# Block-sparse attention and Fourier mixing on one core: idle products before the first scores, first copies of q on ScalarE, and transposes left for the next slot

## Chip, cores and metric

The kernel runs on one core of a Trainium2 chip. The metric is the device time of one execution, in microseconds (us), as the median of three runs.

## The reference, cut to what matters

```python
def _attn_ref(q, k, v, sampled_blocks):          # q, k, v: (4, 8, 768, 64)
    scores = 1/sqrt(64) * np.matmul(q, k.transpose(0, 1, 3, 2))
    # mask: neighbouring blocks of 32, first and last block, 3 sampled blocks a row
    scores = np.where(mask, scores, -1e9)
    attn = softmax(scores)                       # + 1e-9 in the denominator
    return np.matmul(attn, v)

def _moe_ref(x, w_ch1, w_ch2):                   # x: (4, 768, 512)
    mixed = np.real(np.fft.fft(np.fft.fft(x, axis=1), axis=2))
    u = x + mixed
    un = (u - mean(u)) / np.sqrt(var(u) + 1e-6)  # over the last axis
    ch = np.maximum(un @ w_ch1, 0.0) @ w_ch2     # 512 -> 2048 -> 512
    return u + ch

def reference(...):
    attn_out = _attn_ref(q, k, v, sampled_blocks)
    x = attn_out.transpose(0, 2, 1, 3).reshape(4, 768, 512)
    return _moe_ref(x, w_ch1, w_ch2)
```

## The kernel before

The order of instructions on every engine is fixed when the program is generated: the kernel is a Python generator that lays out one static program, and each engine then runs its instructions in that order, waiting where data or a buffer is not there yet. To choose the order, the generator keeps a rough clock of its own (`when`, `free`: estimates in us of when an engine or a PSUM bank is free). These estimates are not times of the chip.

The attention is laid out in slots. A pair of heads `n` takes six slots, `s` = 0 to 5; a batch (four pairs) takes 24, and `r` is the slot's number within the batch. There are 4 x 24 slots and one more for the last remainder. A slot issues the scores of two units (a unit is 128 keys against 384 queries, for two heads), their exponentials, and the products with v of the slot before. In the first batch (`phase` 0) the mask enters as a small extra matmul and the row sums are taken on TensorE (`add_up`); in the later ones VectorE multiplies with a mask and GpSimd adds up. From the second batch on, the Fourier and channel work of the batch before fills TensorE between the slots (`apart`, `late`).

Besides these there are **short steps**: `turn` transposes a piece of q or k on TensorE and copies it out of PSUM; `place` transposes a finished half of the attention output into x; `total` takes row sums; `mask_step` builds a piece of the mask. Nearly all use one of two PSUM tags: `t`, which has a single bank, or `m`, which has two.

The parts that the change and the steps of the prediction touch (cuts marked):

```python
    sum_p = ctx.enter_context(tc.tile_pool(name="sum_p", bufs=1))
    # ... cut ...
    ps_t = ctx.enter_context(tc.tile_pool(name="ps_t", bufs=1, space=PSUM))
    ps_m = ctx.enter_context(tc.tile_pool(name="ps_m", bufs=2, space=PSUM))
    # ... cut ...
    when = {"PE": 0.0, "ACT": 0.0, "DVE": 0.0, "POOL": 0.0}
    free = {"m": [0.0, 0.0], "t": [0.0]}
    # ... cut ...
    def busy(engine, us, after=0.0):
        when[engine] = max(when[engine], after) + us
        return when[engine]
    def bank(tag):
        at = free[tag].index(min(free[tag]))
        when["PE"] = max(when["PE"], free[tag][at])
        free[tag][at] = float("inf")
        return tag, at
    def give(which, at):
        free[which[0]][which[1]] = at + HOP
    # ... cut: a warm-up product, and the first transposes of q and k ...
    def warm(n):
        m = ps_m.tile([P, P], FP32, tag="m", name="warm")
        for _ in range(n):
            nc.tensor.matmul(m, ident, ident, start=True, stop=True)
    # ... cut ...
    def w_round(i):
    # ... cut ...
        nc.scalar.mul(out=lo.bitcast(FP32), in_=lo, mul=2.0 ** -52)
        nc.scalar.mul(out=a.bitcast(FP32), in_=hi.bitcast(FP32), mul=2.0 ** -112)
        nc.vector.tensor_scalar(out=a, in0=a, scalar1=3, scalar2=0x7FFFFFFF,
                                op0=ALU.logical_shift_left, op1=ALU.bitwise_and)
        nc.vector.scalar_tensor_tensor(out=dst.bitcast(U32), in0=hi, scalar=0x80000000, in1=a,
                                       op0=ALU.bitwise_and, op1=ALU.bitwise_or)
        nc.vector.tensor_scalar(out=a, in0=dst.bitcast(U32), scalar1=0xFF800000, scalar2=None,
                                op0=ALU.bitwise_and)
        nc.vector.tensor_mul(out=a.bitcast(FP32), in0=lo.bitcast(FP32), in1=a.bitcast(FP32))
        nc.vector.tensor_add(out=dst, in0=dst, in1=a.bitcast(FP32))
        busy("DVE", 3.0, busy("ACT", 1.2))
    # ... cut ...
    def turn(n, a, half):
        t = loaded[n, a]
        if half == 0:
            turned[n, a] = tp_p.tile([P, S], FP32, tag="qk"[a] + "T", name="qk"[a] + "T")
        dst = turned[n, a]
        first = n == 0 and half == 0
        tag, pool = ("m", ps_m) if first and a == 0 else ("t", ps_t)
        tp, at = pool.tile([P, 512], FP32, tag=tag, name="tp"), bank(tag)
        if a == 0:
            parts = [t[:, c // 2, c % 2, :, :] for c in (range(4, 6) if half else range(4))]
        else:
            parts = [t[:, T * half + c, :, :] for c in range(T)]
        for c, part in enumerate(parts):
            nc.tensor.transpose(tp[:, c * P:(c + 1) * P], part, ident)
        done = busy("PE", 0.15 * len(parts)) + HOP
        if a == 1:
            nc.scalar.copy(out=dst[:, half * HS:(half + 1) * HS], in_=tp[:, 0:HS])
            give(at, busy("ACT", 0.5, done))
        else:
            for i, (to, to_jump, frm, jump, cnt, step) in enumerate(_TURNED[half]):
                on, copy = (("DVE", nc.vector.tensor_copy) if n == 0 and (half == 1 or i % 2 == 0)
                            else ("ACT", nc.scalar.copy))
                copy(out=_grid(dst, to, 2, to_jump, cnt, 1),
                     in_=_grid(tp, frm, 2, jump, cnt, step))
                end = busy(on, 0.27 if cnt > 1 else 0.18, done)
            give(at, end)
        if half == 1:
            flat = t.rearrange("p t r i d -> p (t r i d)" if a == 0 else "p c i d -> p (c i d)")
            nc.scalar.activation(out=flat, in_=flat, func=ACT.Square,
                                 accum_out=peaks[:, 2 * n + a:2 * n + a + 1])
            busy("ACT", 1.05)
    # ... cut ...
    def place(n, half):
        b, j = pairs[n]
        oT = o_of.pop((n, half))
        if j == 0:
            x_of[b, half] = xp.tile([P, T, DM], FP32, tag=("xA", "xB")[half], name="x")
        xt, at = ps_t.tile([P, 512], FP32, tag="t", name="xt"), bank("t")
        for c in range(T):
            nc.tensor.transpose(xt[:, c * P:(c + 1) * P], oT[:, c * P:(c + 1) * P], ident)
        nc.scalar.copy(out=x_of[b, half][:, :, j * P:(j + 1) * P],
                       in_=xt[:, 0:HS].rearrange("p (c f) -> p c f", c=T))
        give(at, busy("ACT", 0.5, busy("PE", 0.45, oT_at[n, half]) + HOP))
    # ... cut ...
    def total(n):
        b, j = pairs[n]
        sp, at = ps_t.tile([P, HS], FP32, tag="t", name="sp"), bank("t")
        for half in range(2):
            acc = acc_of.pop((n, half))
            for i in range(2):
                g = BLK * (2 * half + i)
                nc.tensor.matmul(sp[g:g + BLK, :], pick[:, BLK - j:2 * BLK - j], acc[:, i, :],
                                 start=True, stop=True, tile_position=(0, g))
        into_sums(b, j, sp)
        give(at, busy("DVE", 0.6, busy("PE", 0.7, acc_at[n, 1]) + HOP))
    # ... cut ...
    def gap(rest=0.0, ahead=None, kinds="tm"):
        used = "".join(k for k in "tm" if k not in kinds)
        if ahead is None:
            ahead = AHEAD if late else ALONE
    # ... cut ...
        for item in list(short):
            kind, ready, fn = item
            if kind not in used and max(ready, min(free[kind])) <= when["PE"] + 0.1:
                used += kind
                short.remove(item)
                fn()
    # ... cut ...
    def w_steps(sl):
        while state["w"] < min(len(wchunks), W_PACE * sl):
            w_round(state["w"])
            state["w"] += 1
    def slot(sl):
        phase, r = divmod(sl, SB)
        n, s = divmod(sl, SP)
        units = range(SLOT * sl, SLOT * sl + SLOT)
        if sl < B * SB:
            for u, ps in [(u, scores(u)) for u in units]:
                weigh(u, ps)
        if not late:
            gap(1.5)
        if 0 < sl <= B * SB:
            done = [u - SLOT for u in units]
    # ... cut ...
        reuse = n % NP == 0 and phase >= 2
        if sl > 0 and s == (5 if reuse else 3) and sl <= B * SB:
            b, j = pairs[n]
            at = oT_at[n, 0]
            if reuse:
                until(lambda: (b - 2, 0) in finished)
                at = when["PE"] + LEAVES
            short.append(("t", at, lambda: place(n, 0)))
        if 0 < sl <= B * SB and s == 0 and n % NP != 1:
            short.append(("t", oT_at[n - 1, 1], lambda: place(n - 1, 1)))
        if sl < B * SB and n % NP == 1 and s == 1:
            b = pairs[n - 1][0]
            at = oT_at[n - 1, 1]
            if b >= 2:
                until(lambda: (b - 2, 1) in finished)
                at = when["PE"] + LEAVES
            short.append(("t", at, lambda: place(n - 1, 1)))
        if sl > SB and s == 0 and sl <= B * SB:
            short.append(("t", acc_at[n - 1, 1], lambda: total(n - 1)))
        if n + 1 < len(pairs):
            for at, a, half in ((1, 0, 0), (2, 0, 1), (4, 1, 0), (5, 1, 1)):
                if s == at:
                    short.append(("t", 0.0, lambda a=a, half=half: turn(n + 1, a, half)))
            if s == 1:
                load_v(n + 1)
        if sl == 0:
            short.append(("t", 0.0, lambda: turn(0, 1, 1)))
        if sl == 1:
            short.append(("t", 0.0, lambda: turn(0, 0, 1)))
    # ... cut ...
        if r == 1 and 0 < phase:
            begin(phase - 1)
        # ... cut: filler work of the batch before, each piece followed by gap() ...
        while short and (s in (2, 5) or len(short) > 1 or phase == 0 or sl == B * SB):
            short.popleft()[2]()
    # ... cut ...
        w_loads()
        w_steps(sl)
    # ... cut: the start of the program, after the first loads and the mask's tables ...
    state["got"] = 2
    turn(0, 1, 0)
    turn(0, 0, 0)
    warm(3)
    spread_q(keep_q[0:NB, :], keep)
    w_loads()
    for sl in range(B * SB + 1):
        slot(sl)
```

`gap` issues a short step only where the generator's clock says that its data and its bank are ready; the loop at the end of the slot (line 1238) issues what is left whether it is ready or not. `w_steps` rounds the weights, 1.42 pieces a slot on average: two ScalarE operations and five VectorE operations each, so slot 1 gets two pieces and slot 2 one.

Of the kernel before, what the change touches and what calls it, by code (L numbers as in the profile page):

```python
# [40 lines left out]
def _grid(ap, start, runs, jump, n, step):  # L41

    at = ap[:, start:start + 1]
    return bass.AP(tensor=at.tensor, offset=at.offset,
                   ap=[list(at.ap[0]), [jump, runs], [step, n]])
# [42 lines left out]
def kernel(  # L88
# [14 lines left out]
    nc = tc.nc  # L103

    B, H, S, D = q.shape
# [68 lines left out]
# [16 lines that stand above are left out]
# [29 lines left out]
    def load_v(n, queue=None):  # L219

        b, j = pairs[n]
        vt = ldv.tile([P, 2, C, D], FP32, tag="v", name="vr")
        for i in range(2):
            (queue or nc.sync).dma_start(out=vt[:, i, :, :],
                                         in_=v[b, 2 * j + i].rearrange("(p c) d -> p c d", p=P))
        v_of[n] = vt
# [38 lines left out]
# [5 lines that stand above are left out]
# [163 lines left out]
# [18 lines that stand above are left out]
            give(at, busy("ACT", 0.5, done))  # L451
        else:
            for i, (to, to_jump, frm, jump, cnt, step) in enumerate(_TURNED[half]):
                on, copy = (("DVE", nc.vector.tensor_copy) if n == 0 and (half == 1 or i % 2 == 0)
                            else ("ACT", nc.scalar.copy))
                copy(out=_grid(dst, to, 2, to_jump, cnt, 1),
                     in_=_grid(tp, frm, 2, jump, cnt, step))
# [7 lines that stand above are left out]
# [5 lines left out]
    def scores(u):  # L470
        n, w = divmod(u, UP)
        half, c = divmod(w, C)
        qT, kT = turned[n, 0], turned[n, 1]
        s = ps_s.tile([P, 2, 512], FP32, tag="s", name="s")
        busy("PE", 0.72 if n >= NP else 1.0, max(e_at.get(u - SLOT, 0.0), z_at[u % 2]))
        s_at[u] = when["PE"] + HOP
        for i in range(2):
            nc.tensor.matmul(s[:, i, 0:HS], kT[D * i:D * i + D, c * P:(c + 1) * P],  # L478
                             qT[D * i:D * i + D, half * HS:(half + 1) * HS],
                             start=True, stop=n >= NP)  # L480
        if n < NP:
            for i in range(2):
                nc.tensor.matmul(s[:, i, 0:HS], of_k[D * i:D * i + NB, c * P:(c + 1) * P],  # L483
                                 off_q[D * i:D * i + NB, half * HS:(half + 1) * HS],
                                 start=False, stop=True)
        return s
# [607 lines left out]
    SB = SP * NP  # L1094
    W_PACE = 1.42
    short, apart, late = deque(), deque(), deque()
    state = {"w": 0, "got": 0, "owed": 0.0, "ready": 0.0}

    def channel_step():
        late.popleft()[0]()  # L1100
# [47 lines left out]
    def until(met):  # L1148

        while not met():  # L1150
            if late:
                channel_step()
                gap(2.0)
            else:
                do_apart()
# [21 lines left out]
# [11 lines that stand above are left out]
            for u in done:  # L1188
                values(u)
            if phase == 0 or sl == SB:  # L1190
                add_up(done)
            for u in done:
                e_of.pop(u)
# [30 lines that stand above are left out]
        if phase == 0 and 4 <= sl < 4 + 2 * C:  # L1224
            short.append(("m", 0.0, lambda: mask_step(sl - 4)))
        if r == 1 and 0 < phase:
            begin(phase - 1)
        left = SB * (phase + (0 if r == 0 else 1)) + 1 - sl
        us = sum(step[1] for step in late)
        pace = max(LEAST, min(MOST, (us - COVER) / left)) if left > 0 else MOST  # L1230
        state["owed"] = min(state["owed"], pace) + pace if late else 0.0
        gap(max(state["owed"], 0.0))
        while late and state["owed"] >= late[0][1] / 2:
            state["owed"] -= late[0][1]
            channel_step()
            gap(max(state["owed"], 0.0))

        while short and (s in (2, 5) or len(short) > 1 or phase == 0 or sl == B * SB):
            short.popleft()[2]()
        if s == 3 and n + 2 < len(pairs):  # L1240
            load_q(n + 2)
        if s == 0 and 0 < n < len(pairs) - 1:
            load_k(n + 1)
        w_loads()
        w_steps(sl)
        if sl >= 4 and sl % 2 == 0:
            table_step()
# [21 lines left out]
    state["got"] = 2  # L1269
    turn(0, 1, 0)  # L1270
    turn(0, 0, 0)
    warm(3)
    spread_q(keep_q[0:NB, :], keep)
    w_loads()
    for sl in range(B * SB + 1):
# [112 lines left out]
```

## Time and profile before

| what | value |
|---|---|
| time, three runs | 1108.4, 1109.46, 1109.45 us (median 1109.45) |
| span of the profiled execution | 1109.3 us |
| busy, TensorE matmuls | 1067.7 us (96%) |
| busy, VectorE / ScalarE / GpSimd | 664.8 / 394.1 / 274.2 us |
| granted TensorE clock, mean | 0.994 of full speed |
| matmuls of the warm-up products (line 269) | 18 records, 3.8 us busy |
| first scores begin | 9.16 us |
| first batch of the attention | 9.16 to 133.33 us |

A busy share is an average over the span. What a step costs is read where it stands: from the timeline around it, and from the table of waits, which says for each line of the kernel how long its engine sat idle before it, how often, and which instruction ended the idle time. One call of `warm` leaves two matmul records for each product; a transpose leaves one.

### The profile page before, as it was taken

What the parts mean: (1) busy time and instruction counts of PE and PEld (TensorE: products, weight loads), DVE (VectorE), ACT (ScalarE), POOL (GpSimd) and SP (SyncE); (2) the same over time, 40 slices, a digit from 0 to 9 for tenths busy, and PEclk for the clock granted to TensorE, in tenths of its full rate; (3) what the DMA queues carried; (4) which work ended last, traced back from release to release, by engine and by line L of the source; (5) the groups of instructions that cost most, each with busy time, mean ns of one, the idle gap of its engine ahead of it and who ended that gap; (6) DMA issues with size and microseconds to landing.
All of it is one profiled execution on the core that took longest, in us unless ns stands there. A gap on an engine that the chain in (4) does not pass through costs nothing.

```text
span 1109.3 us, 12468 instructions
## 1 busy us (share of the span) xinstructions
PE 1067.7 (96%) x4446; PEld 544.5 (49%) x4446; DVE 664.8 (60%) x1216; ACT 394.1 (36%) x818; POOL 274.2 (25%) x302
## 2 busy tenths in 40 slices
PE   8999988998899999999999999999999999999996
PEld 3333333544455545444444555454444555568675
DVE  5888878497754525653459355544356446575563
ACT  6788755555212102353443212244330202120210
POOL 1000088688100001245537000344540000000000
PEclk9999999999999999999999999999999999999999
DMA  7756311011000000211110000111000000100001
GB/s 219 208 176 215 93 51 43 15 45 42 1 1 1 0 1 19 66 33 27 43 29 15 1 0 1 51 50 29 1 1 0 1 1 19 39 1 1 1 16 45
DMA packets 65187, 44.30 MB, mean 40 GB/s; under 512 B 52814, under 2 KB 57948, under 8 KB 65116
## 3 DMA queue, kind: packets, MB, share of 16 engines
q1 hardware_dynamic: 63228, 42.62, 13.7%
q10 hardware_dynamic: 1856, 0.79, 0.3%
q8 instruction: 37, 0.61, 0.2%
q14 instruction: 34, 0.28, 0.1%
q0 software_dynamic: 32, 0.01, 0.0%
HBM read 37.11 MB, written 6.29 MB: 39 GB/s over the span
## 4 chain that ended last, share of the span: by engine, by line
PE 85%; DVE 9%; ACT 2%; issue 2%; DMA 0%; POOL 0%; SPq 0%; ACTq 0%; DVEq 0%; POOLq 0%
PE y L954 23%; PE z L898 15%; PE s L478 10%; PE o L522 9%; PE yp L898 7%; PE yy L1017 6%; PE xp L898 4%; DVE e L499 2%; PE tp L447 2%; PE zp L711 1%; PE sp L569 1%; PE zp L682 1%; PE xt L540 1%; PE s L483 1%; PE utp L823 1%
## 5 line engine op out<-in xcount | busy, mean ns | idle before, releaser
L509 POOL TENSOR_TENSOR acc<-acc,e 128x384 f32<-128x384 f32 x192 | 198.3, 1066 | 90.6 <-DVE e L499 90.1
L499 DVE TENSOR_TENSOR e<-s,mask 128x768 f32<-128x768 f32 x144 | 131.2, 951 | 78.4 <-ACT s L497 78.0
L478 PE MATMUL s<-qT,kT 64*128 64x384 f32 x768 | 161.7, 526 | 8.5 <-DVE e L499 7.4
L522 PE MATMUL o<-e,vr 128*64 128x384 f32 x768 | 145.1, 499 | 0.0
L497 ACT ACTIVATE s<-s 128x768 f32<-128x768 f32 x144 | 109.3, 795 | 65.5 <-PE s L478 64.9
L957 DVE TENSOR_TENSOR x<-y,x 128x512 f32<-128x512 f32 x72 | 49.8, 691 | 133.9 <-PE y L954 133.8
L954 PE MATMUL y<-w_sb,hB 128*128 128x512 f32 x288 | 128.4, 595 | 1.1 <-DVE x L957 1.0
L954 PE MATMUL y<-w_sb,hA 128*128 128x512 f32 x288 | 128.8, 594 | 0.6 <-ACT zs L713 0.6
L509 POOL TENSOR_TENSOR acc<-e 128x384 f32<-128x384 f32 x48 | 51.8, 1100 | 231.3 <-DVE e L499 173.2
L903 DVE TENSOR_TENSOR hA<-z,hA 128x384 f32<-128x384 f32 x64 | 35.7, 558 | 111.4 <-PE z L898 111.4
L478 PEld LDWEIGHTS s<-qT,kT 64*128 64x128 f32 x768 | 63.1, 187 | 68.1 <-DVE e L499 25.3
L898 PE MATMUL z<-unT,t 128*128 128x384 f32 x256 | 93.0, 486 | 0.0
L774 POOL TENSOR_SCALAR st<-st 128x1 f32<-128x1 f32 x24 | 6.6, 276 | 344.5 <-DVE st L773 344.1
L954 PEld LDWEIGHTS y<-w_sb,hB 128*128 128x128 f32 x288 | 53.3, 190 | 64.7 <-issue 62.1
L522 PEld LDWEIGHTS o<-e,vr 128*64 128x64 f32 x768 | 46.6, 136 | 73.9 <-issue 71.4
L954 PEld LDWEIGHTS y<-w_sb,hA 128*128 128x128 f32 x288 | 52.9, 190 | 59.6 <-issue 56.6
L907 ACT ACTIVATE hA<-hA 128x384 f32<-128x384 f32 x64 | 33.5, 524 | 123.6 <-DVE hA L903 123.1
L898 PEld LDWEIGHTS z<-unT,t 128*128 128x128 f32 x256 | 48.6, 190 | 33.9
L907 ACT ACTIVATE hB<-hB 128x384 f32<-128x384 f32 x64 | 33.6, 525 | 85.6 <-DVE hB L903 85.6
L898 PE MATMUL z<-t,w_sb 128*128 128x384 f32 x128 | 48.0, 499 | 3.1 <-DVE t L860 3.1
L898 PE MATMUL xp<-unT,w_sb 128*128 128x384 f32 x128 | 47.1, 491 | 1.5 <-ACT zs L713 1.1
L898 PE MATMUL yp<-unT,w_sb 128*128 128x384 f32 x128 | 46.7, 488 | 0.2 <-DVE un L747 0.2
(190 smaller groups left out, 1395.1 us busy)
## 6 DMA issues: line engine op xcount, KB each, us to landing
wraw<-in_moe_w_ch_dram SPq DMA_DIRECT2D x32, 512.0 KB
qr<-in_q_dram SPq DMA_DIRECT2D x90, 64.0 KB
vr<-in_v_dram SPq DMA_DIRECT2D x30, 192.0 KB
kr<-in_k_dram SPq DMA_DIRECT2D x28, 192.0 KB
out_dram<-x SPq DMA_DIRECT2D x16, 128.0 KB
out_dram<-x SPq DMA_DIRECT2D x8, 256.0 KB
out_dram<-x SPq DMA_DIRECT2D x8, 126.0 KB
out_dram<-x SPq DMA_DIRECT2D x4, 252.0 KB
```

Source lines behind the costliest of these rows:

```text
L447: nc.tensor.transpose(tp[:, c * P:(c + 1) * P], part, ident)
L478: nc.tensor.matmul(s[:, i, 0:HS], kT[D * i:D * i + D, c * P:(c + 1) * P], qT[D * i:D * i + D, half * HS:(half + 1) * HS], start=True, stop ...
L497: nc.scalar.activation(out=s[:, :, 0:HS], in_=s[:, :, 0:HS], func=ACT.Exp, scale=scale)
L499: nc.vector.tensor_tensor(out=e, in0=s[:, :, 0:HS], in1=m.broadcast_to([P, 2, HS]), op=ALU.mult)
L509: nc.gpsimd.tensor_add(out=acc, in0=e_of[u - 1][:, i, :] if c == 1 else acc, in1=e[:, i, :])
L522: nc.tensor.matmul(o[D * i:D * i + D, :], vt[:, i, c, :], e[:, i, :], start=(c == 0), stop=(c == C - 1))
L898: nc.tensor.matmul(to, a[:, k, :], c[:, k, :], start=(k == 0), stop=(k == ND // 2 - 1))
L903: tt(out=to, in0=ps, in1=a, op=ALU.add)
L907: nc.scalar.activation(out=h, in_=h, func=ACT.Relu)
L954: nc.tensor.matmul(y, hs[0, half][:, l, m * P:(m + 1) * P], w2_sb[:, 4 * r + l, :], start=(l == 0), stop=(l == 3))
L957: nc.vector.tensor_tensor(out=x[:, m, :], in0=y, in1=x[:, m, :], op=ALU.add)
L1017: nc.tensor.matmul(ps, a[:, k, :], c[k // 2][:, k % 2, :] if isinstance(c, list) else c[:, k, :], start=(k == 0), stop=(k == 3))
```

## The change

Three parts. The second warm-up call issues seven products of the identity with itself in place of three; nothing reads their result, they keep TensorE at work until the first scores can start. The six copies that bring the first half of the first q out of PSUM all go to ScalarE; before, they alternated between VectorE and ScalarE. And the loop at the end of a slot no longer issues a short step that the generator's clock holds to be not ready: it takes ready ones first, and leaves the others for the next slot, except in slots 2 and 5 of a pair and in the first slot of a batch (`r == 0`), where everything left is issued. Before, everything was issued in every slot of the first batch, and in the later batches all but one step (all of them in slots 2 and 5).

```diff
--- before.py
+++ after.py
@@ -451,7 +451,7 @@
             give(at, busy("ACT", 0.5, done))
         else:
             for i, (to, to_jump, frm, jump, cnt, step) in enumerate(_TURNED[half]):
-                on, copy = (("DVE", nc.vector.tensor_copy) if n == 0 and (half == 1 or i % 2 == 0)
+                on, copy = (("DVE", nc.vector.tensor_copy) if n == 0 and half == 1
                             else ("ACT", nc.scalar.copy))
                 copy(out=_grid(dst, to, 2, to_jump, cnt, 1),
                      in_=_grid(tp, frm, 2, jump, cnt, step))
@@ -1235,8 +1235,13 @@
             channel_step()
             gap(max(state["owed"], 0.0))
 
-        while short and (s in (2, 5) or len(short) > 1 or phase == 0 or sl == B * SB):
-            short.popleft()[2]()
+        while short and (s in (2, 5) or len(short) > 1 or phase == 0 or r == 0):
+            ready = [i for i in short if max(i[1], min(free[i[0]])) <= when["PE"] + 0.1]
+            if not ready and s not in (2, 5) and r > 0:
+                break
+            item = ready[0] if ready else short[0]
+            short.remove(item)
+            item[2]()
         if s == 3 and n + 2 < len(pairs):
             load_q(n + 2)
         if s == 0 and 0 < n < len(pairs) - 1:
@@ -1269,7 +1274,7 @@
     state["got"] = 2
     turn(0, 1, 0)
     turn(0, 0, 0)
-    warm(3)
+    warm(7)
     spread_q(keep_q[0:NB, :], keep)
     w_loads()
     for sl in range(B * SB + 1):
```

## The prediction

> **What bounds the kernel now.** I read the page's totals first, then TensorE's table of waits, then the timeline of all engines around each wait that belongs to a short step. From the page:
>
> ```profile
> PE 1067.7 (96%) x4446; PEld 544.5 (49%) x4446; DVE 664.8 (60%) x1216; ACT 394.1 (36%) x818; POOL 274.2 (25%) x302
> PE 85%; DVE 9%; ACT 2%; issue 2%; DMA 0%; POOL 0%; SPq 0%; ACTq 0%; DVEq 0%; POOLq 0%
> ```
>
> TensorE (PE) works 1067.7 of 1109.3 us and carries 85% of the chain that ended last. Its work is not touched except for the warm-up products, so a change of order can win or lose only in the 41.6 us of idle time. The table of waits, TensorE alone (total us, times, longest):
>
> ```profile
> PE s L478 <- DVE e L499: 7.4, 10, 2.2
> PE xt L540 <- ACT oT L528: 4.1, 5, 1.0
> PE tp L447 <- ACT qT L456: 3.4, 3, 1.1
> PE z L898 <- DVE t L860: 3.1, 1, 3.1
> ...
> PE xt L540 <- DVE sums L551: 1.3, 1, 1.3
> ...
> PE s L478 <- ACT qT L456: 0.9, 1, 0.9
> ...
> PE xt L540 <- DVE r L599: 0.6, 1, 0.6
> ```
>
> Lines 540 and 447 are `place` and `turn`, the steps that may now be left: the whole stake of the third part is some 10 us, under 1%. Line 478 behind q's copies (0.9) is the stake of the other two. The timeline of all engines at the start, where the change does most (start, duration, engine, line):
>
> ```profile
> 8.00 0.29 DVE L456 COPY qT<-tp 128x128 f32<-128x128 f32 x1
> 8.32 0.27 ACT L456 COPY qT<-tp 128x128 f32<-128x128 f32 x1 [1.49 <-DVE qT L456]
> 8.62 0.29 DVE L456 COPY qT<-tp 128x126 f32<-128x126 f32 x1 [0.33 <-ACT qT L456]
> 8.95 0.16 ACT L456 COPY qT<-tp 128x2 f32<-128x2 f32 x1 [0.35 <-DVE qT L456]
> ...
> 17.01 1.03 ACT L456 COPY qT<-tp 128x128 f32<-128x128 f32 x6 [1.99 <-PE tp L447]
> 18.09 0.44 PE L447 MATMUL tp<-ident,qr 128*128 128x128 f32 x2 [1.12 <-ACT qT L456]
> 18.56 0.56 DVE L456 COPY qT<-tp 128x128 f32<-128x128 f32 x3 [7.51 <-PE tp L447]
> 19.40 0.65 ACT L410 ACTIVATE wraw<-wraw 128x512 f32<-128x512 uint32 x1
> 20.63 0.43 DVE L414 TENSOR_SCALAR wraw<-wraw 128x512 uint32<-128x512 uint32 x1 [1.51 <-ACT wraw L413]
> ```
>
> The first four show that copies shared between two engines take turns; the last five are slot 1: q of pair 1 leaves the `t` bank, the second half of q of pair 0 follows after 1.12 us of waiting, VectorE copies it at once, and only then do both engines begin to round weights.
>
> **What the Trainium skill says.** "PSUM — Partial Sum Buffer", section "PSUM bank collisions raise a hardware error", says that two engines' accesses to one bank and quadrant must be kept apart, reads too; the trace agrees: no two of the first copies overlap. The same page, "Engine vs sequencer instructions", has the queues of VectorE and ScalarE strictly first in, first out, with matmuls in program order; the trace shows it in TensorE standing still for one transpose while the next scores' data are there. "Perfetto Trace Analysis", "Matmuls", advises rotating PSUM banks so that one is emptied while the next fills; tag `t` has one, and the 1.12 us is the price. "TensorE: Matmul & The Clock Gate", "What's actually happening", says that an idle window of about 3.4 us halves the clock. Here less is enough: after a wait of 2.18 us at 248.85 the records show a granted clock of 0.50.
>
> ```profile
> 190.31 2.69 PE L478 MATMUL s<-qT,kT 64*128 64x384 f32 x8 [1.31 <-DVE e L499]
> 248.85 2.93 PE L478 MATMUL s<-qT,kT 64*128 64x384 f32 x8 [2.18 <-DVE e L499]
> ```
>
> The same eight matmuls take 1.78 us after short waits.
>
> **Part 1 and 2, the start.** q's transposes end at 7.17 + 0.41 = 7.58. ScalarE is free from 6.84 (its copy of k), while VectorE is held by the mask until 7.97, so all six copies can start at 7.62. In slot 1 the same six take 1.03 us on ScalarE, and the four that the first scores need are done 0.76 after the start by the chain of waits: 7.62 + 0.76 = 8.38, against 8.95 + 0.16 = 9.11 before. But the seven products are now in front: six records took 0.83 us from 7.42, with 0.27 for a single one, so one starts every 0.112, and fourteen hold TensorE until 7.42 + 1.57 = 8.99. The scores start there instead of at 9.16: **-0.17 us**, with the products and not the copies setting it. No clock was lost at the old gap (four score matmuls take 0.92 before and after), so the products bring nothing else.
>
> **Part 3, slots 1 and 2: a loss.** In slot 1 two steps want `t`: q of pair 1, then the second half of q of pair 0. The second is not ready by the generator's clock, so it is left for slot 2, behind slot 1's two weight pieces on VectorE. Scores of slot 2 start at 16.73 instead of 18.45 (the next instruction after the transposes at 16.31, where four leave after 0.59, minus 0.17). ScalarE's first weight operation moves from 19.40 to 18.04 - 0.17 = 17.87, so by 1.53. VectorE's two pieces ran from 20.63 to 26.67 with hardly a gap; they now end at 26.67 - 1.53 = 25.14. Then come the three copies (0.56), at 25.70, and only then TensorE's next transposes (q of pair 1, second half, forced in slot 2, same bank) and the scores of slot 3, which read that very half of q. With 0.05 to the start and 0.36 to the next instruction, as at 18.09, slot 3 begins at 26.1 where it began at 23.27: **+2.8 us**, the start's gain and the 1.12 of slot 1 included.
>
> TensorE's own work of slot 2 ends near 16.73 + 4.45 + 0.36 = 21.5 (4.45 is 18.45 to 22.90 before, 0.36 the added transposes). It then stands still for 25.75 - 21.5 = 4.2 us, so the clock will fall. At 190.31 that cost 2.69 - 1.78 for the scores and 1.36 - 0.85 for the sums after them, 1.4 in all; at 248.85 1.3. I take **+1.4**. Slot 3 stands at +4.2.
>
> **Part 3, the rest of the first batch: gains.** Four forced waits go: 0.31 at 48.86 (slot 7), 0.87 at 60.18 (slot 9), 0.98 at 107.15 (slot 18), 0.99 at 123.00 (slot 21). Each such step is taken up between scores and values of the next slot, where its data are over 2 us old. TensorE is busy 116.6 of the 121 us from 9 to 130, VectorE and ScalarE 96 each, so this is kept: **-3.15**.
>
> **Part 3, later batches.** Slot 31 (168.18) loses a wait of 1.35, but its two steps go to slot 32 together with a third, and there a pair is forced one after the other, at the 1.12 seen at 18.09 and 147.80: -0.2. Slot 36 (188.45, 0.64): TensorE next waits 1.31 for VectorE's e until 190.31, so nothing is gained. In slots 48 and 72 (`r == 0`) everything must now be issued: in 48 `total` follows `place` and waits for ScalarE's copy that ends at 255.64, while TensorE is free at 255.06: +0.6. In 72 `place` waits for the sums on VectorE that end at 580.49, while TensorE is free at 579.71: +0.8, and the 0.62 at 583.82 goes: +0.2. The waits at 147.80 and 264.07 stand in slots with s = 2, that at 702.13 with s = 5, and those at the end of the last batch were forced already: unchanged. Sum **+0.6**.
>
> Total: 4.2 - 3.15 + 0.6 = +1.7, so 1109.45 + 1.7 = **1111.1 us**.
>
> **Rivals.** (a) Slot 2 costs little: VectorE reaches the copies sooner than I hold, or the step is taken ahead of the weights. For it: VectorE is idle 7.5 us before 18.56. Against: that idle time lies before the weights in program order, and the queue keeps its order. Without the loss and the clock the sum is about -0.17 - 1.12 - 3.15 + 0.6 = -3.8, near 1106. (b) Weights arrive late or the backlog grows: the 40 us from 20 keep the DMA queues 0.67 busy and ScalarE 33.5 us; a later piece or a new wait in slots 5, 11 or 23, where a step left over meets one that is forced, gives 1 to 2 us more, 1113. (c) VectorE becomes the bound: it is busy 41.0 of the 50 us from 130 and TensorE waits for e there. Then a shift of 1 us in the first batch is partly swallowed, up or down, and the time stays at 1109 to 1110.
>
> **Range and chances.** The large terms are two opposite ones of 4.2 and 3.2 us; the first may be a third smaller, a wait or two of the second may return, and runs differ by 1.1. That gives 1108.0 to 1113.5. The 2% line is 22 us away, twice all waits of the short steps: within 2% is nearly sure.
>
> **What would show it.** Right: first scores near 9.0; six copies on ScalarE in a row; in slot 2 a TensorE wait of some 4 us, ended by VectorE's copies of q (line 456), slot 3 near 26, and a granted clock of 0.5 for some 3 us behind it; no `place` waiting for oT at 60, 107 and 123; a wait of 0.6 to 0.8 before `total` in slot 48 and `place` in slot 72. Wrong: no long wait ahead of slot 3 (then rival a), or new waits of `turn` in slots 5, 11, 23 (b), or waits for e from 130 on that differ by more than 1 us (c).

## The result, and the profile after

The changed kernel takes 1116.31 us (median of four runs, 1113.6 to 1118.13) against 1109.45: **0.6% slower**, ratio 1.0062 with a 95% interval of 1.0041 to 1.0084. The prediction was 1111.1, with a range of 1108.0 to 1113.5: the direction and the class (within 2%) hold, the size does not, and the measured time lies above the range.

The page of the changed kernel, the rows of busy time and of the chain:

```profile
PE 1075.7 (96%) x4454; PEld 547.6 (49%) x4454; DVE 662.2 (59%) x1213; ACT 393.6 (35%) x821; POOL 273.6 (25%) x302
PE 86%; DVE 8%; issue 2%; ACT 2%; POOL 1%; DMA 1%; SPq 0%; DVEq 0%; POOLq 0%; ACTq 0%
```

The chain that ended last still runs on TensorE (PE), now for 86% of the span. TensorE has eight records more, the four added products, about 0.9 us by the prediction's 0.112 a record. Yet it is busy 8.0 us longer: the same matmuls ran longer, so a clock must have fallen. The page's mean granted clock says so: 0.986, against 0.994 before. Of the span's 7.1 us of growth (1116.4 against 1109.3), idle time has no part; it shrank by 0.9. TensorE's table of waits (total us, times, longest) of the changed kernel shows why: waits were exchanged.

```profile
PE s L478 <- DVE e L499: 9.2, 9, 2.5
PE tp L447 <- issue: 4.9, 2, 4.0
...
PE tp L447 <- ACT qT L456: 2.2, 2, 1.1
PE xt L540 <- DVE sums L553: 1.7, 2, 0.9
...
PE xt L540 <- ACT oT L528: 0.6, 1, 0.6
```

`place` behind oT (line 540) fell from 4.1 us to 0.6. In its stead stand one wait of 4.0 us before a transpose of q, and 1.8 us more of waiting for VectorE's e. The long one, in the timeline of all engines (start, duration, engine, line):

```profile
8.34 0.92 PE L478 MATMUL s<-qT,kT 64*128 64x384 f32 x4
...
18.35 0.43 DVE L414 TENSOR_SCALAR wraw<-wraw 128x512 uint32<-128x512 uint32 x1 [8.62 <-ACT wraw L413]
...
23.70 0.69 DVE L422 TENSOR_TENSOR w_sb<-w_sb,wraw 128x512 f32<-128x512 f32 x1
...
24.31 0.55 DVE L456 COPY qT<-tp 128x128 f32<-128x128 f32 x3
...
24.96 0.66 PE L447 MATMUL tp<-ident,qk 128*128 128x128 f32 x2 [3.99 <-issue]
...
25.55 1.65 PE L478 MATMUL s<-qT,kT 64*128 64x384 f32 x4
...
33.78 0.94 PE L478 MATMUL s<-qT,kT 64*128 64x384 f32 x4
```

Read from the end: TensorE stood still 3.99 us before the transposes at 24.96. The view names "issue" as the releaser, which only says that it found no semaphore event to blame. The lines above tell more: VectorE's three copies of q end at 24.86, 0.1 us earlier, and empty the very bank. They stand behind an unbroken row of weight roundings from 18.35. The four score matmuls that follow take 1.65 us instead of 0.92. The clock, in windows of the same kernel (next to last but two columns: the granted clock):

```profile
23.00:24.00 1.00, 0.00 (x0) 0.00 (x0) 0.97 (x2) 0.00 (x0) 0.00 (x0) 0.81 0.84 312
...
33.00:34.00 1.00, 1.00 (x10) 0.22 (x4) 0.09 (x1) 1.00 (x3) 0.00 (x0) 0.57 0.92 348
34.00:35.00 1.00, 1.00 (x8) 0.28 (x6) 0.96 (x3) 1.00 (x3) 0.00 (x0) 1.00 0.12 45
```

A mean of 0.81 in the first microsecond means that the clock fell to a half at about 23.62 (0.38 us at half speed); 0.57 in the second that it came back at 33.86. It was halved for 10.24 us, and all of slot 3 ran in it. There is a second place of loss, at the border between the first two batches, in TensorE's timeline of the changed kernel:

```profile
141.91 2.24 PE L478 MATMUL s<-qT,kT 64*128 64x384 f32 x8 [1.51 <-DVE e L499]
...
153.28 0.67 PE L447 MATMUL tp<-ident,qr 128*128 128x128 f32 x2 [1.12 <-ACT qT L456]
153.87 2.93 PE L478 MATMUL s<-qT,kT 64*128 64x384 f32 x8
```

Before, the wait of slot 25 (here at 141.91) was 0.48, and these groups took 1.78 and 1.56 us. The start of each slot's scores gives the account of the two profiled executions:

| point | before | after | difference | step from the row above |
|---|---|---|---|---|
| slot 0 | 9.16 | 8.34 | -0.82 | -0.82 |
| slot 3 | 23.27 | 25.55 | +2.28 | +3.10: the wait in slot 2, less the 1.12 of slot 1; 0.2 for its transposes at half clock |
| slot 6 | 38.58 | 44.66 | +6.08 | **+3.80**: halved clock in slot 3 |
| slot 24 | 133.33 | 136.14 | +2.81 | -3.27: forced waits gone |
| slot 30 | 159.89 | 166.42 | +6.53 | **+3.72**: border of the batches |
| end | 1109.3 | 1116.4 | +7.1 | +0.6: later batches |

### The profile page after: what moved, and what is told of

Read it like the earlier page. It is cut to its first block, busy times and chain, and to the rows that moved or that the text cites. A ratio compares the mean times of both kernels' runs of the same rounds, so it can differ in the third digit from the quotient of the medians. Undisturbed runs are those within 1.5% of the kernel's fastest.

```text
span 1116.4 us, 12487 instructions
## 1 busy us (share of the span) xinstructions
PE 1075.7 (96%) x4454; PEld 547.6 (49%) x4454; DVE 662.2 (59%) x1213; ACT 393.6 (35%) x821; POOL 273.6 (25%) x302
## 4 chain that ended last, share of the span: by engine, by line
PE 86%; DVE 8%; issue 2%; ACT 2%; POOL 1%; DMA 1%; SPq 0%; DVEq 0%; POOLq 0%; ACTq 0%
PE y L954 22%; PE z L898 15%; PE s L478 11%; PE o L522 9%; PE yp L898 7%; PE yy L1017 6%; PE xp L898 4%; DVE e L499 2%; PE tp L447 2%; PE zp L711 1%; PE sp L569 1%; PE zp L682 1%; PE xt L540 1%; PE s L483 1%; PE utp L823 1%
## 5 line engine op out<-in xcount | busy, mean ns | idle before, releaser
L478 PE MATMUL s<-qT,kT 64*128 64x384 f32 x768 | 164.8, 535 | 9.4 <-DVE e L499 9.2
L522 PE MATMUL o<-e,vr 128*64 128x384 f32 x768 | 148.1, 507 | 0.0
L898 PE MATMUL z<-t,t 128*128 128x384 f32 x128 | 46.9, 490 | 0.0
```

What stands on the lines that cost most here:

```text
L522: nc.tensor.matmul(o[D * i:D * i + D, :], vt[:, i, c, :], e[:, i, :], start=(c == 0), stop=(c == C - 1))
L898: nc.tensor.matmul(to, a[:, k, :], c[:, k, :], start=(k == 0), stop=(k == ND // 2 - 1))
```

## The experiments

All ratios are to the kernel before, run on the same chip alongside, with 95% intervals; times are medians, with the range of the runs. The chips differ from one group of experiments to the next (medians of the kernel before: 1109.45 to 1111.4 us), so across groups the ratios compare better than the times. In the expectations, theory C says that the loss comes from VectorE's queue ahead of q's copies and from the halved clock behind that wait, and theory B that a row of VectorE work at the end of the first batch takes gains back; a rival is the other outcome.

### 1. Products in the gap of slot 2

Is the clock the dear part of slot 2, or the wait itself? Sixteen idle products fill TensorE's idle time ahead of the transposes; the wait for VectorE stays.

```diff
# the kernel after
+        if sl == 2:
+            warm(16)
         while short and (s in (2, 5) or len(short) > 1 or phase == 0 or r == 0):
```

> The changed kernel with 16 idle products ahead of the forced transposes of slot 2, so that TensorE works through most of its 4.0 us wait; the wait itself, VectorE's order and everything else stay. Theory C (the halved clock after that wait costs as much as the wait): slot 3's scores take 0.92 us per four matmuls and not 1.65, slot 6 begins some 3.8 us earlier than the 44.66 of the changed kernel, and the median falls from 1116.3 to about 1112.5; if the first batch's end waits on VectorE's backlog, part of it is given back there and it is 1113 to 1115. Rival D (only the delay of VectorE's weights by the long wait counts): slot 24 begins where it did and the median stays at 1116.

Measured: 1112.16 us (1109.98 to 1114.9), ratio 1.0009 [0.9997, 1.0022]. TensorE's timeline of this kernel:

```profile
25.75 0.41 PE L447 MATMUL tp<-ident,qk 128*128 128x128 f32 x2 [0.22 <-issue]
26.09 0.92 PE L478 MATMUL s<-qT,kT 64*128 64x384 f32 x4
```

Slot 3 starts no earlier (26.09), but its scores take 0.92 us again, and slot 4 follows 4.45 us later, where it took 8.23 after the change: 3.8 us were clock. The median is 4.15 us below that of the changed kernel, and the ratio falls from 1.0062 to 1.0009. The wait of 1.51 us in slot 25 is still there (138.63), so it does not come from the clock of slot 3.

### 2. Half as many products

> The changed kernel with 8 idle products ahead of slot 2's forced transposes, so that some 2.2 us of the 4.0 us wait are idle. Theory C: the delay is the same, and the clock halves for at most one stretch of 3.4 us: median 1111 to 1114, between the 1112.2 with 16 products and the 1116.3 of the changed kernel. Rival: any wait over about 1.5 us costs the same and the median is 1116.

The same with `warm(8)`: 1111.89 us (1109.92 to 1114.34), ratio 0.9997 [0.9969, 1.0024]. TensorE's timeline:

```profile
25.56 0.41 PE L447 MATMUL tp<-ident,qk 128*128 128x128 f32 x2 [2.01 <-issue]
25.90 0.92 PE L478 MATMUL s<-qT,kT 64*128 64x384 f32 x4
```

2.0 us of idle time are left, and the clock does not fall: slot 4 again follows 4.45 us later. Half of the products were enough here, with some luck: where in time the 2.0 us lay mattered too, as the part on why the prediction failed shows.

### 3. Slot 1 issues everything

The new loop stays; slot 1 alone is excepted, so that the second half of q goes ahead of the weights again.

```diff
# the kernel after
-            if not ready and s not in (2, 5) and r > 0:
+            if not ready and s not in (2, 5) and r > 0 and sl != 1:
```

> The changed kernel, but slot 1 issues all its short steps as before (the second half of the first q is not left for slot 2); everything else of the change stays. Theory C: no 4 us wait, no halved clock before slot 24; the first batch gains the start (0.2 to 0.8) and the four waits (3.2), so slot 24 would begin near 129.5 against 133.33 before. The median is 1107 to 1108 if that gain is kept; if VectorE's backlog of weights sets the first masked e (rival D), slot 25 begins no earlier than about 137 and the median is 1109 to 1112, with a wait for e of 3 us or more and a halved clock after it. If neither holds and the loss sits in the later batches' order, it stays above 1114.

Measured: 1109.35 us (1108.36 to 1111.12), ratio 0.9992 [0.9979, 1.0005]. Slot 3 starts at 23.44, at full clock, and slot 24 at 130.22, so 3.11 earlier than before: the waits of slots 7, 9, 18 and 21 are gone as in the changed kernel. Not all of that lasts, because of slot 25:

```profile
135.99 1.78 PE L478 MATMUL s<-qT,kT 64*128 64x384 f32 x8 [1.50 <-DVE e L499]
```

Slot 30 starts at 157.79, 2.10 us ahead of before: 1.0 us of the gain is given back in this wait, with no halved clock here. The profile keeps 1.9 us to its end (span 1107.4 against 1109.3); over all runs the interval of the ratio includes 1.

### 4. The start alone, and the loop alone

```diff
# the start alone: the kernel after with the old loop
-        while short and (s in (2, 5) or len(short) > 1 or phase == 0 or r == 0):
-            ready = ...                                  # cut: the new loop's body
+        while short and (s in (2, 5) or len(short) > 1 or phase == 0 or sl == B * SB):
+            short.popleft()[2]()
```

> Only the start of the change: seven idle products, q's six first copies on ScalarE; the old loop. Both theories: the first scores begin at 8.3 to 9.0 us against 9.16, nothing else moves, the median is 1108.6 to 1109.3.

Measured: 1109.76 us (1107.57 to 1112.66), ratio 0.9992 [0.9978, 1.0006]: no difference that can be told.

```diff
# the loop alone: the kernel after with the old start
-                on, copy = (("DVE", nc.vector.tensor_copy) if n == 0 and half == 1
+                on, copy = (("DVE", nc.vector.tensor_copy) if n == 0 and (half == 1 or i % 2 == 0)
...
-    warm(7)
+    warm(3)
```

> Only the loop of the change: short steps that are not ready are left; three idle products and alternating copies as before. Both theories: slot 2's wait of some 4 us and the halved clock are there, the median is 1116 to 1118, so the loop alone carries the loss. If it were under 1112, the start would have a part in it.

Measured: 1117.77 us (1116.53 to 1124.12), ratio 1.0075 [1.0055, 1.0095]. The wait before the transposes is 3.98 us (at 25.78), the clock is halved from 25.7 to 32.5. The loss is the loop's.

### 5. One step alone

Is it the new loop as a whole, or the one step of slot 1? The kernel before, with its old loop, leaves only this step for slot 2.

```diff
# the kernel before
         while short and (s in (2, 5) or len(short) > 1 or phase == 0 or sl == B * SB):
+            if sl == 1 and len(short) == 1:
+                break
             short.popleft()[2]()
```

> The kernel before, with a single step moved: the second half of the first q is left for slot 2, behind slot 1's two weight pieces on VectorE; nothing else of the change. Theory C: this one step carries the whole loss, slot 3 begins near 26.3 instead of 23.3, behind a wait of about 4 us, with the clock halved for 2 or 3 stretches of 3.4 us (1.7 us of work lost in each), so the median is 1116 to 1118 against 1110.95 before on this chip. Rival D (the loss is shared with the other moved steps): under 1114.

Measured: 1116.35 us (1114.31 to 1120.09), ratio 1.0037 [1.0009, 1.0066]; on this chip the runs of the kernel before spread from 1109.43 to 1117.25, so the interval is wide. The profile is plain:

```profile
25.78 0.41 PE L447 MATMUL tp<-ident,qk 128*128 128x128 f32 x2 [3.99 <-issue]
```

The wait is 3.99 us again, and slot 4 begins at 34.18 where it was 28.20, slot 24 at 139.26 where it was 133.33. One step out of 25 slots carries +5.9 us. The wait of slot 25 stays at 0.48, for in this kernel slot 21 still waits (0.98 us at 128.92), so no gain has to be given back.

### 6. The same order, with the copies on ScalarE

If the loss comes from VectorE's queue, then TensorE's order of the changed kernel is harmless once the copies of the second half stand in another queue. One condition is taken out, so that `turn` copies every piece of q on ScalarE.

```diff
# the kernel after
-                on, copy = (("DVE", nc.vector.tensor_copy) if n == 0 and half == 1
-                            else ("ACT", nc.scalar.copy))
+                on, copy = ("ACT", nc.scalar.copy)
```

> The changed kernel with the three copies of the second half of the first q on ScalarE instead of VectorE; TensorE's order is that of the changed kernel. Theory C (the wait was VectorE's queue, not the step's later place): the 4 us wait shrinks to under 0.6 us, slot 3 begins near 22.5, no halved clock there; the wait for e at slot 25 stays 1.5 us; median 1107 to 1109. Rival D (the later place itself costs): a wait of 2 us or more remains ahead of slot 3 and the median stays over 1112.

Measured: 1108.88 us (1106.05 to 1110.9), ratio 0.9961 [0.9934, 0.9987]. TensorE's timeline:

```profile
22.38 0.44 PE L447 MATMUL tp<-ident,qk 128*128 128x128 f32 x2 [0.35 <-ACT qT L456]
```

The wait of 3.99 us is 0.35, slot 3 starts at 22.75. TensorE's order is that of the changed kernel, only the engine of three copies differs: the queue in front of the copies was the cause. Slot 24 starts at 129.53, and slot 25 waits 1.51 us.

### 7. Slot 21 alone

Where is the gain given back? In the profile before, VectorE rounds weights (and copies a few tables) from 120.06 to 137.09, 17.0 us without a gap, and the first e of slot 25 stands behind them; TensorE waits for it:

```profile
120.06 0.43 DVE L414 TENSOR_SCALAR wraw<-wraw 128x512 uint32<-128x512 uint32 x1 [2.04 <-ACT wraw L413]
...
137.09 1.80 DVE L499 TENSOR_TENSOR e<-s,mask 128x768 f32<-128x768 f32 x2
138.08 1.78 PE L478 MATMUL s<-qT,kT 64*128 64x384 f32 x8 [0.48 <-DVE e L499]
```

A step that is taken earlier on TensorE in slot 21 (123.00) can't shorten that row. In this run the kernel before leaves only the short step of slot 21.

```diff
# the kernel before
-        while short and (s in (2, 5) or len(short) > 1 or phase == 0 or sl == B * SB):
+        while short and sl != 21 and (s in (2, 5) or len(short) > 1 or phase == 0 or sl == B * SB):
```

> The kernel before with a single step moved: place of slot 21, whose wait of 0.99 us ended at 123.00, is left for slot 22; VectorE's order is untouched. Theory B: the wait goes, and comes back as a wait for e at slot 25 that grows from 0.48 to about 1.5 us; slot 25 begins where it did, the median within 0.5 us of before, or up to 2 us over it if the clock halves after the longer wait. Rival (the gain is kept): slot 25 begins 1 us earlier and the wait there stays 0.5.

Measured: 1111.13 us (1109.63 to 1113.91), ratio 0.9987 [0.9972, 1.0002]. TensorE's timeline:

```profile
139.58 1.78 PE L478 MATMUL s<-qT,kT 64*128 64x384 f32 x8 [1.51 <-DVE e L499]
```

The scores of slot 21 start at 119.03, 1.54 us later than in the profile before, those of slot 22 at 123.48, only 0.01 later: 0.99 us of waiting is gone, and the transposes' 0.48 us now stand in slot 22. VectorE's row begins 1.54 us later too and keeps its length: it runs from 121.60 to 138.59, 17.0 us. In slot 25 the lag is 1.50 again (139.58 against 138.08). The wait there went from 0.48 to 1.51, by 1.03, and the gain of slot 21 is given back whole.

The lag has a source of its own. With three products TensorE waits for the copies at the start (before: 0.91 us), in this profile for 1.97 us, and the first two groups of scores then take 1.58 and 1.65 us in place of 0.92: the clock was halved there too. In none of the nine profiles with seven products do these groups take more than 0.92.

### 8. A shorter row on VectorE: the attempt that went wrong

To see whether the row's length sets the wait, the last two VectorE operations of pieces 26 to 31 go to GpSimd, in the kernel of experiment 3.

```diff
# the kernel of experiment 3, in w_round
-        nc.vector.tensor_mul(out=a.bitcast(FP32), in0=lo.bitcast(FP32), in1=a.bitcast(FP32))
-        nc.vector.tensor_add(out=dst, in0=dst, in1=a.bitcast(FP32))
+        last_ops = nc.gpsimd if i >= 26 else nc.vector
+        last_ops.tensor_mul(out=a.bitcast(FP32), in0=lo.bitcast(FP32), in1=a.bitcast(FP32))
+        last_ops.tensor_add(out=dst, in0=dst, in1=a.bitcast(FP32))
```

> The changed kernel with slot 1 issuing all its steps (as in the earlier run), and the last two of five VectorE operations of weight pieces 26 to 31 on GpSimd, idle at that time; this takes 6 x 1.38 = 8.3 us off VectorE before slot 24. Theory B (VectorE's unbroken queue from slot 21 on holds back the first masked e): the wait for e at slot 25 falls from 1.50 to under 0.3 us, the median falls by 1.0 to 1.5 us against that earlier run's 1109.35. Rival: the wait at slot 25 has another cause and stays at 1.5; or VectorE's next waits swallow it and the median stays within 0.5 of 1109.35.

Measured: 1113.79 us (1112.07 to 1114.1), ratio 1.001 [0.9984, 1.0035]. The row became longer, 18.7 us, and the wait of slot 25 with it: 3.25 us in place of 1.50. The timeline of this kernel shows how:

```profile
118.59 0.69 DVE L416 SCALAR_TENSOR_TENSOR w_sb<-wraw 128x512 uint32<-128x512 uint32 x1
...
119.88 1.35 POOL L422 TENSOR_TENSOR wraw<-wraw 128x512 f32<-128x512 f32 x1 [2.23 <-DVE wraw L419]
...
120.11 1.67 DVE L416 SCALAR_TENSOR_TENSOR w_sb<-wraw 128x512 uint32<-128x512 uint32 x1
```

The same VectorE operation takes 0.69 us alone and 1.67 beside GpSimd's; line 419 goes from 0.43 to 1.38. The Trainium skill's "SBUF — State Buffer", section "Who interferes with whom", says that a VectorE operation with two SBUF inputs contends with a GpSimd one that reads SBUF; line 416 has two such inputs, and the trace agrees. Line 419 has one; why it stretches too was not tested. The expected gain did not come, but the point stands with the opposite sign: a row 1.7 us longer gave a wait 1.75 us longer.

### 9. Weights one piece ahead

The row can also be shortened, by rounding one of its pieces before it begins. From slot 9 on, one more piece than the pace asks for is rounded, on top of experiment 6.

```diff
# the kernel of experiment 6, in w_steps
-        while state["w"] < min(len(wchunks), W_PACE * sl):
+        while state["w"] < min(len(wchunks), W_PACE * sl + (sl > 8)):
```

> The changed kernel with the second half of the first q copied by ScalarE (as in the earlier run), and the weight pieces one ahead from slot 9 on, so that VectorE has one piece (3.0 us) less in its unbroken queue after slot 20. Theory B: the wait for e at slot 25 falls from 1.5 to under 0.5 us, and the median is about 1 us under the earlier run's 1108.9. Rival: ScalarE, busy nearly all of slots 20 to 22, sets the queue's start, and the wait stays over 1 us.

Measured: 1107.31 us (1105.12 to 1108.24), ratio 0.9958 [0.9944, 0.9971]. The row is 14.1 us long in place of 17.0 (117.14 to 131.24), and slot 25 follows slot 24 at 133.55 without a wait. A new one of 0.27 us stands at 73.80. That the median is 1.6 us below experiment 6's is no proof by itself, as the ranges of the runs overlap; the wait that went is.

### 10. Known waits covered with products

Three waits of more than 2 us remain with the new loop: slots 37 and 48 (2.48 and 2.17 us), and the first product of the channel work (2.3). Eight idle products go ahead of each, on top of experiment 9; they start no data earlier, they only keep TensorE at work. Not every kernel lost clock in all three places: experiment 3 lost none behind slot 48.

```diff
# the kernel of experiment 9
+            if b == 0 and p == 0:
+                warm(8)                 # ahead of the first z product
...
+        if sl in (36, 47):
+            warm(8)                     # ahead of the loop at the slot's end
```

> The run with the weights ahead, and 8 idle products (1.8 us) ahead of each of the three waits of 2.2 to 2.5 us that halve the clock in every kernel so far: ahead of the scores of slots 37 and 48, and of the first sum of the first channel product. Theory C: the waits stay, the clock stays full there, each saves 1.0 to 1.7 us: median near 1104. Rival: the halved stretches are covered by later waits for VectorE, and the median stays within 1 us of the run without the products.

Measured: **1102.86 us** (1102.77 to 1103.93), ratio 0.9919 [0.9906, 0.9933], the fastest of all and, by the ratios, faster than both kernels. First a line of the timeline of experiment 9, then two of this kernel:

```profile
276.75 2.53 PE L898 MATMUL z<-t,w_sb 128*128 128x384 f32 x4 [2.30 <-DVE t L860]
```

```profile
274.28 1.95 PE L269 MATMUL warm<-ident 128*128 128x128 f32 x16
...
276.74 1.56 PE L898 MATMUL z<-t,w_sb 128*128 128x384 f32 x4 [0.52 <-DVE t L860]
```

The product starts at the same moment, 276.75 and 276.74, but takes 1.56 us in place of 2.53. The granted clock of the five runs is 0.996 at the median (0.996 to 0.998) against 0.992 (0.992 to 0.994) in experiment 9. 0.004 of a span of 1105 us is 4.4 us, and the medians lie 4.45 apart. The clock is given in thousandths only, so this is agreement to about 1 us. The spread of the runs fell from 3.1 to 1.2 us. Place by place only the third is shown: in the profile of experiment 9, the fastest of its runs, the clock did not fall behind the waits of slots 37 and 48 either (eight score matmuls take 1.78 us at 186.60 and at 244.20), and the two profiles' spans differ by 1.7 us (1103.4 and 1101.7), all of it at the third place. That the other runs lost the rest in the first two is likely, but not recorded.

## Why the prediction failed, step by step

| term of the sum | predicted | measured |
|---|---|---|
| start (part of the next row) | -0.17 | -0.82 in the profile; -1.33 to +0.29 over nine kernels |
| slot 3, start and wait together | +2.8 | +2.28 |
| halved clock behind that wait | +1.4 | **+3.80** |
| forced waits of the first batch | -3.15 | -3.27 |
| border of the batches | 0 | **+3.72** |
| later batches | +0.6 | +0.6 |
| sum | +1.7 (rounded) | +7.1 |

**What held.** The step of slot 1 fell behind the weights as worked out: a wait of 3.99 us (4.2 predicted), ended by VectorE's copies of q, slot 3 at 25.55 or, with the old start, 26.36 (26.1 predicted). Experiment 6 shows the cause by changing only the engine of those copies, and experiment 5 that this one step carries the loss. The four forced waits went (`place` behind oT: 4.1 to 0.6), and in the later batches the waits of 0.66 in slot 48 and 0.85 in slot 72 stand where 0.6 and 0.8 were predicted. Rival (a), that slot 2 costs little, fell with the 3.99 us. So did (b): between 25 and 141 us TensorE's timeline shows no wait, nor one in slots 5, 11 or 23.

That the later batches sum to +0.6 as predicted is in part luck. Slots 30 to 40 cost 0.59 (-0.2 predicted), slots 40 to 53 only 0.27 (+0.6 predicted for slot 48), the first channel work gained 0.46 (not predicted), and slot 72 cost 0.19 (+0.2 predicted).

**The start** has the predicted form, six copies in 1.03 us on ScalarE and the products setting the first scores, but not a fixed time. In nine kernels with seven products the scores begin between 7.83 and 9.45, in four with three products at 9.16. Two things vary. One is the load of q, for which TensorE waited 0.43 and 0.45 us in experiments 1 and 3, not at all in the changed kernel, and 0.59 in the profile before, which the prediction carried over:

```profile
7.17 0.41 PE L447 MATMUL tp<-ident,qr 128*128 128x128 f32 x2 [0.59 <-DMA qr<-in_q_dram]
```

The other is the fourteen records of the products, taken as 1.57 us: they took 1.73 in the changed kernel and up to 2.67 (experiment 6), there at a granted clock of 1.00, from a cause that stays open. So the -0.82 of one profile says little about what the start is worth. The start alone (experiment 4) gains nothing that can be told from zero. "The products bring nothing else" was too short, though: the profile of experiment 7 has a halved clock behind the gap that they fill.

**First failed step: "I take +1.4".** It was read off single halved stretches of about 3.4 us behind waits of 1.3 and 2.2 us. That the clock would fall was right, but behind 4 us of idle time the halved stretch was 10.24 us in the changed kernel and 6.8 with the loop alone: three times and twice 3.4. The whole of slot 3 fell in it, 4.45 us of work becoming 8.23. The Trainium skill's "TensorE: Matmul & The Clock Gate", "What's actually happening", counts in free-running windows of 3.4 us and lets the clock return after one busy window or more. The multiples agree with such windows. But TensorE worked without a wait from 24.96 to the clock's return at 33.86, 8.9 us, so here one busy window was not enough. The step should have been the slot's work at half speed, some 4 us; measured were 3.80.

**Second failed step: "this is kept".** The argument was the mean load of the first 130 us (VectorE 96 of 121). A mean hides the end of the batch, where VectorE has no gap for 17 us. The 0.99 us gained in slot 21 lies inside that row and was given back in slot 25; experiment 7 shows it alone, 8 that the row's length sets the wait, 9 that a row one piece shorter removes it. This is rival (c) in part: VectorE is the bound there, and takes back 1.03 us. The other 2.7 us of the border are again clock, two halved stretches of 3.4 us, at 143.1 and 153.3. They are not a fixed price of the longer wait: experiments 2 and 3 have the same wait and no halving there, while experiments 9 and 10 have one halved stretch, from 144.1 and 143.8, without that wait. The profiled execution is also the slowest of the four (span 1116.4; the others 1111.8 to 1114.7, at a clock of 0.989); behind which waits the clock fell in those others is not recorded.

Why the same wait is followed by a fall of the clock to one half in one profile and not in the next can be read from the traces. The six falls of the changed kernel's profile (23.63, 143.09, 153.33, 197.71, 255.73 and 289.87) lie 35, 3, 13, 17 and 10 times 3.413 us apart, as if the clock were set on a fixed grid of such windows. On that grid, laid through each profile's falls, TensorE's idle time within one window tells the falls apart. Between 5 and 320 us of all thirteen profiles, windows at half clock left out, all 43 with 1.90 us or more of idle time ended in a fall, none with less than 1.50 did, and 4 of 11 between. So a wait of 2.0 to 2.5 us can be cut by a window's edge and pass. The 2.48 us at 186.60 in experiment 9 lay as 0.91 and 1.58 in two windows and no clock fell; in the changed kernel they lay in one, and the score matmuls took 2.49 us. The 2.01 us of experiment 2 lay as 1.31 and 0.70. A wait of 4 us has about 2 us or more in one window wherever the edge lies. At the border, the waits of 0.87 and 1.12 us (151.53 and 153.28) shared one window in the changed kernel and lay in two in the profile before, without a fall. The other fall there ended a window with 1.51 us of idle time, the longer wait of slot 25, as against 1.50 without a fall in experiment 3. So the 2.7 us of clock at the border are largely chance, and the 3.80 behind slot 2 are not.

What stays open: why the clock stayed low through a window in which TensorE had 0.12 us of idle time or less (27.04 to 30.45 in the changed kernel, likewise one in experiments 4 and 5 each), while behind the other 44 falls it came back after one window. Not tried: letting the first slot of a batch leave its steps too, as its steps belong to the batch that ends there.

## What to carry to other kernels

Before a step is left for a later place, look at what its consumer engine has queued ahead of that place: here a readiness rule on TensorE's side put three copies (0.56 us in all) behind 6 us of weight rounding. Price a TensorE wait of about 2 us or more with the risk that the work behind it runs at half clock (here 1.3 to 1.7 us for each stretch of 3.4 us, and up to three stretches behind 4 us), and where the wait can't be removed, cover it with idle products that end just before the data arrive (8 products three times lowered the median by 4.45 us here). A gain on one engine that lies inside another engine's unbroken row is given back at that row's end, so count gains only up to the next such row.

## What was not expected of the hardware

- The clock came back after 3.4, 6.8 or 10.24 us, in steps of one length, and in three kernels later than one stretch of full work.
- A fall is not certain: behind the same wait of slot 48, 2.17 us, the eight score matmuls take 2.93 us in the changed kernel and 1.78 in experiment 3. In the first, 1.95 us of idle time lay in one window of 3.41 us, in the second 1.79.
- GpSimd's 128x512 operations more than doubled the VectorE operations beside them (0.69 to 1.67, 0.43 to 1.38 us), so moving work off VectorE lengthened VectorE's row.
